# Attention values of a tile in two neighbouring PSUM banks, normalised in one step, with smaller key and value rings and a new instruction order

## The chip, the core and the metric

The kernel runs on one core of a Trainium2 chip. The metric is the device time of one execution in microseconds (us). The engines are TensorE (PE, matrix products into PSUM), VectorE (DVE), ScalarE (ACT), GpSimd (POOL, here mostly the issuer of loads that convert float32 to bfloat16 on the way) and SyncE (SP, here the issuer of transposing DMAs and of stores). They run side by side, each in the order of its own instruction stream, and wait for each other by semaphores.

## What is computed

```
scores = scale * q @ k.T                     # (4, 8, 768, 768), head size 64
keep   = is_global | is_local                # first 8 keys, or the last 96 positions
a      = softmax(where(keep, scores - slope[h] * dist, -1e9))
x      = (a @ v).transpose(0, 2, 1, 3).reshape(3072, 512)
out    = relu(x @ w_in) ** 2 @ w_out         # w_in 512 x 2048, w_out 2048 x 512
```

## The kernel before

**Tiles and blocks.** The 4 x 768 positions make 24 tiles of 128 rows (`j`), six to a batch; two tiles make a block of 256 rows (`blk`, 12 of them). The local window of 96 positions means that a tile meets only itself, the tile before it and 8 global keys.

**Attention of a tile.** Loads of q, k and v come from POOL (lines 330 and 334). For tiles 0 to 7 PE transposes q and k (`tr`, line 528) and ACT or DVE copies them out of PSUM (`T`, lines 453 and 455); from tile 8 on SP issues a transposing DMA (`T`, line 554). `sc` (line 618) makes the scores with 64-row products; tiles 6 and 7, 12 and 13, 18 and 19 are made in one go. `exp` (ACT, line 684) leaves PSUM, `mul` (DVE, line 709) applies mask and slope, `pv` (PE, line 767) multiplies by v. One `pv` is half a tile, four heads, in one PSUM bank of 4 x 65 columns; the 65th column of a head is the sum that the softmax divides by. `norm` (DVE, lines 797 and 798) is a reciprocal of four sums and a multiply of 4 x 64 values for each half, so two of each in a tile; it writes `x`. Then x is transposed, by PE for tiles 0 to 7 (`trx`, line 835) and by a DMA from SP after that (`xT`, line 859).

**The two layers.** Block 0 and half of block 1 go through `s1` (plain products with w_in, line 1081). The other blocks use a scheme with seven products in place of eight (`first_seven`, line 917): `xs` makes differences of halves of xT on DVE (line 939), `h` are the seven products of a half block (p1 to p7, line 967, eight matmuls each), `u` copies partial sums out of a bank that the next product then adds to, `c` adds them up and clips them at zero, `q` squares into `hs`. The second layer (`seven`) does the same with sums `sum` (line 1185), products `s2` (line 1230, four matmuls each piece), copies `part`, results `o` (line 1305) and stores `st` (line 1327).

**What sets the order.** `ORDER` is a long string. A word is an operation, `@A` or `@V` puts a choice of engine on ACT or DVE, and the digits after the colon are the PSUM banks. `Plan.run` emits the operations in that order, and each engine keeps its part of it. Operations also name buffers of rings: eight banks, 16 work buffers `buf`, `xT` 3, `hs` 3, `x` 2, transposed keys and queries `qkT` 12 (`NKT`), values 10 (`NV`). Three ring slots hold q and k from tile 6 on. A load of tile j from tile 9 on waits, by a small memset on DVE (`gate`, line 502), until the value slot that it takes has been read.

Of the kernel before, what the change touches and what calls it, by code (L numbers as in the profile page):

```python
# [62 lines left out]
trx.1:6 exp.3.0.1 exp.3.1.0:7 exp.3.0.0 ld.win.1.0 pv.2.0:2 pv.2.1:5 norm.2.0:0 norm.2.1 gv.2@V mul.3.0:8 sc.4.0:1037
exp.4.1.0:9 trx.2:2 ld.win.4.0 xT.1@A exp.4.1.1:a tr.1.5:4 tr.0.5:5 T.1.5@A exp.4.0.0 xT.2@A:1 mul.3.1:b pv.3.0:0
pv.3.1:6 T.0.5@A s1.0.1:7 norm.3.0:1 gk.4@V exp.4.0.1 norm.3.1 gv.3@A s1.0.1#2 trx.3:4 sc.5.0:0126 exp.5.0.1:c
exp.5.1.0:d s1.0.4:5 exp.5.1.1 E0.0 mul.4.0:e xT.3@V ld.v.4 mul.4.1:f ones.6 pv.4.0:3 s1.1.1:4 relu.0.4@V:2 exp.5.0.0
ld.win.3.0 s1.0.3:2 pv.4.1:1 relu.0.1@A:0 sq.0.1@A:0 gv.4@A s1.0.3#2 mul.5.1:1 s1.1.3:6 norm.4.0:0 norm.4.1 ld.win.2.0
ld.win.0.0 s1.0.0:5 relu.0.3@A:3 sq.0.3@A mul.5.0:5 gate.10 s1.0.2:0 trx.4:7 relu.1.1@A:4 sq.1.1@A:1 xs.1.0:0 ld.v.5
ld.win.2.1 pv.5.0:3 ld.win.0.1 pv.5.1:1 xs.1.1 ld.win.6.0 ld.win.7.0 ld.win.5.0 relu.1.3@A:7 norm.5.0:1 norm.5.1
ld.wout.3 s1.1.2:2 xT.4@A:2 relu.1.2@A:8 ld.wout.2 ld.wout.1 ld.wout.0 isum.0.0 s1.1.0:4 s1.0.2#2 trx.5:3 gate.14  # L70
xT.5@V relu.1.0@A:6 sq.1.2@A s1.0.0#2 xs.2.0:1 h.2.0.p1:1 sq.1.0@V sq.0.4@A u.2.0.1@A:b isum.3.0 sq.1.3@A xs.2.1
ld.wout.7 isum.0.1 s1.0.0#3 s1.0.6:6 gate.11 isum.1.0 isum.1.1 xs.1.2 s1.0.7:7 h.2.0.p2:2 c.2.0.c11:9 h.2.1.p1:3
# [5 lines left out]
h.1.1.p4 h.2.0.p4 wsum.0.1 s2.1.p1.0:0 T.8 c.2.0.c21@A:6 h.2.0.p3 h.2.1.p4 s2.0.p1.0:7 h.1.1.p3 sum.0.1 s2.0.p2.0:4
q.1.1.c22@A q.1.1.c11@A s2.0.p1.1 q.2.1.c22@A:2 q.2.0.c11@A part.0.p1@A:0 c.1.1.c21@A:c s2.0.p2.1 s2.1.p1.1 wsum.1.1
s2.0.p6.0 s2.0.p6.1 c.1.1.c12:7 tr.1.6:1 tr.0.6:6 part.1.p1@A:1 q.1.1.c21@A s2.1.p2.0:2 q.2.1.c11@A sum.0.3 wsum.2.1  # L80
part.0.p6@A:2 o.0.p2:a c.2.1.c21@A:2 s2.1.p2.1 wsum.3.1 wsum.3.0 T.1.6@V s2.0.p7.0 s2.0.p7.1 gate.12 s2.0.p5.0
q.1.1.c12@A s2.0.p5.1 c.2.0.c12:e load.9 part.0.p7@A:3 q.2.1.c12@A T.0.6@A q.2.0.c22@A o.0.p5:d s2.0.p4.0 s2.0.p4.1
q.2.0.c12@A o.0.p4@A sum.1.0:1 s2.0.p3.0 tr.0.7:3 gate.13 sum.1.1 s2.0.p3.1 o.1.p2:0 o.0.p3 sum.1.2 T.0.7@A tr.1.7:1
sum.2.2:0 sum.1.3 sum.2.0 T.1.7@A q.2.0.c21@A s2.1.p6.0 s2.1.p6.1 q.2.1.c21@A part.1.p6@A:0 sc.6.0:567341 exp.6.1.0:3
load.10 gk.7@A exp.6.0.0 s2.1.p5.0 s2.1.p7.0 s2.1.p7.1 mul.6.0:b exp.7.0.0:9 exp.7.1.0 part.1.p7@A:3 s2.2.p1.0:6
s2.1.p5.1 sum.2.1 exp.7.0.1:1 exp.7.1.1 o.1.p5:c mul.7.0:5 s2.2.p1.1 pv.6.0:5 norm.6.0:0 s2.1.p4.0 s2.1.p4.1 o.1.p4@A
pv.6.1:7 s2.1.p3.0 sc.8.0:3415 exp.8.0.1:7 part.2.p1@A:1 pv.7.0:0 s2.1.p3.1 mul.7.1:8 norm.6.1 T.9 pv.7.1:7 norm.7.0:1
norm.7.1 trx.6:1 exp.8.1.0:4 xT.6@V:0 exp.8.1.1 exp.8.0.0 s2.2.p6.0 s2.2.p6.1 o.1.p3 gate.15 trx.7:0 xT.7@A gk.8@V
mul.8.1:f h.3.1.p1:4 u.3.1.1@A:e gv.7@V h.3.0.p2:7 sc.9.0:5132 exp.9.0.1:6 exp.9.1.0:2 xs.3.0:0 xs.3.1 exp.9.0.0
h.3.0.p1:0 h.3.1.p6 mul.8.0:3 s2.2.p2.0:3 u.3.0.1@V:9 pv.8.0:1 u.3.1.2@A:b T.10 c.3.0.c11:1 h.3.0.p6 pv.8.1:5  # L90
norm.8.0:0 exp.9.1.1 sum.2.3 norm.8.1 xs.3.2 part.2.p6@A:2 xT.8:2 s2.2.p2.1 h.3.1.p7 h.3.1.p5:7 u.3.0.2@A:5
u.3.1.3@A:8 c.3.1.c22:7 o.2.p2:4 mul.9.0:3 mul.9.1:9 h.3.0.p7 s2.2.p7.0 s2.2.p7.1 u.3.0.3@A:f q.3.1.c22@A:0
part.2.p7@A:3 q.3.0.c11@A h.3.0.p5:2 h.3.1.p2:1 c.3.1.c11:8 gv.8@V load.11 c.3.0.c22:7 h.3.1.p3 h.3.0.p4 c.3.0.c21@A:2
h.3.1.p4 c.3.1.c21@A:1 q.3.1.c11@A c.3.1.c12:6 s2.2.p5.0 pv.9.0:5 gk.9@V T.11 st.0.0 norm.9.0:1 q.3.1.c12@A
q.3.0.c22@A h.3.0.p3 pv.9.1:1 gv.9@A c.3.0.c12:e norm.9.1 s2.3.p1.0:0 s2.2.p5.1 sc.10.0:4752 exp.10.1.1:f h.4.0.p1:1
s2.2.p4.0 exp.10.1.0:3 s2.2.p4.1 q.3.0.c12@V s2.3.p1.1 sum.3.0:1 o.2.p5:b s2.2.p3.0 s2.2.p3.1 exp.10.0.1 exp.10.0.0
part.3.p1@A:0 sum.3.1 h.4.1.p1:2 s2.3.p6.0 o.2.p4@A mul.10.0:8 s2.3.p6.1 sum.3.2 pv.10.0:7 mul.10.1:9 o.2.p3 gk.10@A
xT.9 norm.10.0:0 xs.4.0:1 xs.4.1 h.4.1.p2:5 pv.10.1:4 q.3.1.c21@A q.3.0.c21@A part.3.p6@A:1 u.4.1.1@A:6 u.4.0.1@A:5
s2.3.p7.0 s2.3.p7.1 h.4.1.p6 u.4.1.2@A:7 norm.10.1 h.4.0.p6 u.4.0.2@A:e gate.18 sc.11.0:6374 exp.11.1.0:a exp.11.0.0
gv.10@V c.4.1.c11:3 part.3.p7@V:3 sum.3.3 xs.4.2 load.12 h.4.0.p2:5 T.12 exp.11.1.1:1 h.4.1.p7 s2.3.p4.0 mul.11.0:2  # L100
exp.11.0.1 c.4.0.c11:f u.4.1.3@A:8 mul.11.1:9 load.13 h.4.0.p7 h.4.1.p5:3 c.4.1.c22:6 s2.3.p2.0:6 pv.11.0:4
u.4.0.3@A:a norm.11.0:1 q.4.1.c11@A:1 h.4.1.p4 h.4.0.p5:7 c.4.0.c22:5 s2.3.p2.1 o.3.p2:2 pv.11.1:5 q.4.1.c22@A
h.4.1.p3 q.4.0.c11@A gate.16 norm.11.1 h.4.0.p4 c.4.1.c21@A:1 c.4.0.c21@A:3 h.4.0.p3 s2.3.p4.1 c.4.1.c12:8 q.4.1.c12@A
c.4.0.c12:6 T.13 s2.3.p5.0 s2.3.p5.1 o.3.p5:9 q.4.0.c22@A q.4.0.c21@A o.3.p4@A sc.12.0:425137 exp.12.0.0:a st.2.1
exp.12.1.0 exp.13.0.0:b exp.13.1.0 exp.13.0.1:f q.4.0.c12@V s2.3.p3.0 sum.4.2:0 sum.4.0 xT.10:1 h.5.1.p1:0 s2.3.p3.1
mul.12.0:7 s2.4.p1.0:4 xT.11 o.3.p3 gate.19 xs.5.0:0 xs.5.1 h.5.0.p1:2 u.5.0.1@A:e q.4.1.c21@A h.5.1.p2:5 s2.4.p1.1
sum.4.1 part.4.p1@A:2 u.5.1.1@A:8 load.15 load.14 st.2.0 st.3.1 h.5.0.p5:1 pv.12.0:6 h.5.0.p6 mul.13.0:5 h.5.0.p2:3
c.5.0.c11:3 norm.12.0:0 s2.4.p6.0 xs.5.2 u.5.0.2@A:6 exp.13.1.1 mul.13.1:a q.5.0.c11@A:2 h.5.1.p6 h.5.0.p7 pv.12.1:7
u.5.0.3@A:4 s2.4.p2.0:3 s2.4.p6.1 s2.4.p2.1 pv.13.0:6 c.5.0.c22:1 gk.13@V h.5.0.p3 u.5.1.2@A:9 c.5.1.c11:b h.5.0.p4
norm.13.0:1 q.5.0.c22@A part.4.p6@A:0 norm.12.1 pv.13.1:5 norm.13.1 o.4.p2:e h.5.1.p7 gate.21 c.5.0.c12:3 h.5.1.p5:6  # L110
s2.4.p7.0 s2.4.p7.1 c.5.0.c21@A:7 q.5.0.c21@A u.5.1.3@A:f load.16 st.1.0 T.14 q.5.1.c11@V c.5.1.c22:0 h.5.1.p4 T.15
sum.4.3 T.16 sc.14.0:7251 xT.12:0 gv.13@A xT.13 q.5.1.c22@V q.5.0.c12@A s2.4.p5.0 part.4.p7@A:3 gate.17 exp.14.1.0:4
# [1337 lines left out]
```

## Time and profile before

| | |
|---|---|
| timed runs | 197.23 us median of 3 (196.97 to 197.88) |
| span of the profiled execution, first to last instruction | 195.7 us |
| PE busy | 188.5 us, 2808 matmuls |
| DVE busy | 179.4 us, 437 instructions |
| ACT busy | 161.6 us, 338 instructions |
| granted TensorE clock | 1.00 throughout |

The profiled execution's own total is not listed beside its span; the median of the timed runs is 1.5 us more than the span, and this is taken as what lies around it. A view "by line" groups equal instructions: busy time, mean duration of one, and how long the engine stood idle before them and for whom. In the timeline and in the chain a row begins with start and duration in us. Matmul records overlap, so that a busy PE need not be one that issues without a gap; a group's pace is read from starts.

### The profile page before, as it was taken

What the parts mean: (1) busy time and instruction counts of PE and PEld (TensorE: products, weight loads), DVE (VectorE), ACT (ScalarE), POOL (GpSimd) and SP (SyncE); (2) the same over time, 40 slices, a digit from 0 to 9 for tenths busy, and PEclk for the clock granted to TensorE, in tenths of its full rate; (3) what the DMA queues carried; (4) which work ended last, traced back from release to release, by engine and by line L of the source; (5) the groups of instructions that cost most, each with busy time, mean ns of one, the idle gap of its engine ahead of it and who ended that gap; (6) DMA issues with size and microseconds to landing.
All of it is one profiled execution on the core that took longest, in us unless ns stands there. A gap on an engine that the chain in (4) does not pass through costs nothing.

```text
span 195.7 us, 6835 instructions
## 1 busy us (share of the span) xinstructions
PE 188.5 (96%) x2808; PEld 170.5 (87%) x2808; DVE 179.4 (92%) x437; ACT 161.6 (83%) x338; POOL 75.1 (38%) x93
## 2 busy tenths in 40 slices
...
GB/s 125 149 150 167 179 193 205 205 162 151 155 150 143 99 177 168 119 100 227 139 79 129 138 74 119 209 168 97 147 113 188 85 136 13 20 193 105 0 91 234
DMA packets 111713, 26.92 MB, mean 138 GB/s; under 512 B 103234, under 2 KB 108866, under 8 KB 111682
## 3 DMA queue, kind: packets, MB, share of 16 engines
...
q8 instruction: 22, 0.36, 0.7%
...
## 4 chain that ended last, share of the span: by engine, by line
PE 85%; POOL 6%; DMA 5%; DVE 1%; issue 0%; POOLq 0%; DVEq 0%
PE bank L1230 37%; PE bank L967 32%; PE bank L1081 6%; PE bank L618 5%; PE bank L767 5%; POOL qk_first L330 5%; DMA win<-in_moe_w_in_dram 3%; DMA xT<-x 2%; POOL v L330 2%; PE bank L835 1%; PE bank L528 0%; DVE xs L939 0%; DVE buf L886 0%; DVE hsum L1185 0%; DVE early L1305 0%
## 5 line engine op out<-in xcount | busy, mean ns | idle before, releaser
L684 ACT ACTIVATE buf<-bank 128x512 bf16<-128x512 f32 x76 | 41.5, 613 | 2.8 <-PE bank L618 2.7
L1031 ACT ACTIVATE hs<-buf 128x512 bf16<-128x512 f32 x62 | 37.2, 635 | 2.5 <-DVE buf L1011 2.0
L1230 PEld LDWEIGHTS <-hsum 128*128 128x128 bf16 x384 | 35.3, 98 | 4.0
L453 ACT COPY buf<-bank 128x512 f32<-128x512 f32 (+1 forms) x59 | 32.1, 569 | 7.7 <-PE bank L967 6.1
L1230 PE MATMUL bank<-wsum,hsum 128*128 128x256 bf16 x288 | 38.0, 273 | 0.0
L1011 DVE CUSTOM_DVE_ANT_0 buf<-bank,buf 128x512 f32<-128x512 f32 x49 | 33.0, 682 | 0.8 <-ACT buf L453 0.3
L967 PEld LDWEIGHTS <-qk_first 128*128 128x128 bf16 x504 | 31.1, 98 | 1.4 <-issue 0.3
L967 PEld LDWEIGHTS <-win 128*128 128x128 bf16 x504 | 30.8, 98 | 0.9
L334 POOL DMA_DIRECT2D qk<-in_q_dram x18 | 16.0, 889 | 35.3 <-DMA qkT<-qk 30.0
L1230 PEld LDWEIGHTS <-hs 128*128 128x128 bf16 x288 | 26.3, 98 | 2.7
L1230 PE MATMUL bank<-wout,hs 128*128 128x256 bf16 x192 | 27.3, 273 | 0.0
L334 POOL DMA_DIRECT2D v<-in_v_dram x18 | 16.0, 891 | 23.1 <-PE bank L967 13.1
L967 PE MATMUL bank<-xs,qk_first 128*128 128x128 bf16 x336 | 24.6, 219 | 0.2 <-DVE buf L886 0.2
L967 PE MATMUL bank<-xT,win 128*128 128x128 bf16 x336 | 24.6, 219 | 0.0
L709 DVE TENSOR_TENSOR buf<-buf,E 128x1024 bf16<-128x1024 bf16 x32 | 21.5, 683 | 0.5 <-ACT buf L684 0.5
L798 DVE TENSOR_TENSOR x<-bank,rs 128x256 bf16<-128x256 f32 x48 | 20.4, 425 | 1.7
L767 PE MATMUL bank<-v,buf 128*128 128x65 bf16 x312 | 16.1, 193 | 0.9 <-DMA v<-in_v_dram 0.5
L1185 DVE TENSOR_TENSOR hsum<-hs 128x1024 bf16<-128x1024 bf16 (+1 forms) x26 | 16.4, 642 | 0.3
L334 POOL DMA_DIRECT2D qk<-in_k_dram x18 | 16.1, 897 | 0.6 <-DMA wout<-in_moe_w_out_dram 0.4
L767 PEld LDWEIGHTS <-buf 128*128 128x128 bf16 x312 | 13.9, 98 | 1.8 <-DVE buf L709 0.6
L884 ACT ACTIVATE buf<-bank 128x512 f32<-128x512 f32 x23 | 13.7, 607 | 1.0 <-PE bank L967 1.0
L453 ACT COPY part<-bank 128x256 f32<-128x256 f32 x29 | 11.1, 383 | 3.6 <-PE bank L1230 3.6
...
## 6 DMA issues: line engine op xcount, KB each, us to landing
...
```

The source lines that it names most:

```text
L334: nc.gpsimd.dma_start(out=dst, in_=src)
L453: nc.scalar.copy(dst, src)
L684: nc.scalar.activation(out=tiles[tag, j, g][:, odd], in_=tiles.pop(("sc", j, odd, g)).rearrange("p a c -> p (a c)"), func=Act.Exp, scale=s ...
L709: nc.vector.tensor_mul(at, tiles.pop(("esc", j, g)), bias)
L767: nc.tensor.matmul(out=po[:, hi, :], lhsT=tiles["at", j, g][:, odd, at * P : (at + 1) * P], rhs=v_sb[kj][:, h, :], start=(i == 0), stop=(i ...
L798: nc.vector.tensor_tensor(out=x[:, 4 * hf : 4 * hf + 4, :], in0=po[:, :, :D], in1=rs.to_broadcast([P, 4, D]), op=Alu.mult,)
L884: nc.scalar.activation(dst, src, Act.Relu)
L967: nc.tensor.matmul(out=tiles["h", blk, g, bank][:, n], lhsT=left_[:, s, k], rhs=right_[:, k], start=opens and n == 0 and k == 0, stop=k == ...
L1011: nc.vector._custom_dve(TENSOR_ADD_SAT, out=hr, in0=src, in1=tiles.pop(("u", blk, g, i)), s0=float("inf"), s1=0.0,)
L1031: nc.scalar.activation(hs, hr, Act.Square)
L1185: nc.vector.tensor_tensor(out=t[:, i, h], in0=t[:, a, h] if isinstance(a, int) else half_a(blk, *a)[:, h], in1=t[:, b, h] if isinstance(b, ...
L1230: nc.tensor.matmul(out=tiles["acc", blk, bank][:, cols], lhsT=left_[:, s], rhs=right_[:, cols], start=first and s == 0, stop=s == NSTEP - ...
```

## The change

1. `pv` of both halves of a tile takes two neighbouring banks at once (all banks are now one PSUM tile), and one `norm` follows: a reciprocal of 8 sums and a multiply of 8 x 64 values, read across the two banks. Both banks stay taken until it is through.
2. `NKT` goes from 12 to 9 and `NV` from 10 to 9; `hs` and `xT` rings go from 3 to 4 buffers.
3. `ORDER` is another string: the order of all operations, the choices of engine and the banks.
4. `first_seven` can take two blocks at a time; with `PAIRS` empty this isn't used, and its products are as before.

```diff
-    NQ, NKT, NV = 3, 2 * TPB, 10
+    NQ, NKT, NV = 3, 9, 9
-    banks = [ps.tile([P, 4 * P], FP32, name=f"bank_{i}", tag=f"bank_{i}") for i in range(NBANK)]
+    bank_all = ps.tile([P, NBANK, 4 * P], FP32, name="bank", tag="bank")
+    banks = [bank_all[:, i] for i in range(NBANK)]
-    NHB = 3
+    WHOLE = True
+    PAIRS = ()
+    NHB = 4
+    NXT = 4
...
-                po = psum()[:, : 4 * (D + 1)].rearrange("p (a c) -> p a c", a=4)
+                if hf == 0 and WHOLE:
+                    assert given[1] == given[0] + 1
+                    tiles["po", j] = bank_all[:, given[0] : given[0] + 2, : 4 * (D + 1)].rearrange("p b (a c) -> p b a c", a=4)
+                po = tiles["po", j][:, hf] if WHOLE else psum()[:, : 4 * (D + 1)].rearrange("p (a c) -> p a c", a=4)
...
+            def emit_whole(e, j=j):
+                tiles["x", j] = lent("x")
+                x, po = tiles["x", j], tiles.pop(("po", j))
+                rs = work.tile([P, 2, 4, 1], FP32, name="rs", tag="rs")
+                nc.vector.reciprocal(rs, po[:, :, :, D : D + 1])
+                nc.vector.tensor_tensor(
+                    out=x.rearrange("p (b a) c -> p b a c", b=2),
+                    in0=po[:, :, :, :D],
+                    in1=rs.to_broadcast([P, 2, 4, D]),
+                    op=Alu.mult,
+                )
```

The order of the start in both, from the first operation to the first one with w_in (`ld` is a load's issue on POOL, `s1.0.1` the first product with w_in):

```diff
-tr.0.0:0 T.0.0@V tr.1.0:1 bias.0.0:23 T.1.0@V ld.q.1 ld.k.1 tr.0.1:4 T.0.1@V ld.q.2 ld.k.2 E0.1 ld.q.3 ld.v.0 ld.k.3
-tr.1.1:5 T.1.1@A ld.v.1 sc.0.0 bias.1.0:6701 exp.0.1.0:0 sc.1.0 tr.0.2:4 exp.0.0.0 gk.1@A T.0.2@V exp.1.0.0:1 tr.1.2:5
...
+tr.0.0:0 T.0.0@A tr.1.0:1 bias.0.0:23 T.1.0@A ld.q.1 tr.0.1:0 ld.k.1 tr.1.1:4 T.1.1 T.0.1 sc.0.0 exp.0.0.0:0 exp.0.1.0
+bias.1.0:1567 sc.1.0 gk.1 exp.1.0.0:1 E0.1 ld.q.2 ld.v.0 tr.0.2:3 T.0.2 ld.k.2 tr.1.2:2 T.1.2 pv.0.0:01 pv.0.1 norm.0:0
+exp.1.1.0 exp.1.1.1:3 ld.k.4 tr.1.4:5 T.1.4 exp.1.0.1 bias.2.0:4372 ones.6 sc.2.0 exp.2.0.0:2 ld.q.3 tr.0.3:5 T.0.3
+exp.2.1.0 trx.0:0 xT.0:0 gk.2@A exp.2.0.1:0 ld.k.3 tr.1.3:1 T.1.3 exp.2.1.1 ld.v.1 pv.1.0:45 pv.1.1 norm.1:0 sc.3.0:1036
+exp.3.1.0:3 ld.q.4 tr.0.4:7 T.0.4 gv.1 ld.v.2 pv.2.0:45 pv.2.1 gk.3 exp.3.0.0 mul.3.0:1 exp.3.0.1:4 exp.3.1.1 norm.2:1
+gv.2 ld.q.5 ld.k.5 trx.1:1 xT.1@A sc.4.0:3702 exp.4.1.1:3 exp.4.0.0:0 tr.0.5:6 T.0.5 tr.1.5:1 ld.v.3 gk.4@A exp.4.0.1
+trx.2:4 xT.2@A:1 pv.3.0:56 mul.3.1:2 pv.3.1 T.1.5 sc.5.0:1032 exp.5.0.0:2 exp.4.1.0 ld.win.1.0 s1.0.1:4 ld.win.3.0
+norm.3:1 trx.3:5 xT.3 s1.0.1#2
```

The new order of PE and SP around three later places that the prediction speaks of (other engines left out; a word without a piece number stands for one piece of four matmuls of `s2` or eight of `h`):

```
tile 9:   tr.1.6 tr.0.6 tr.1.7 s2.0.p4 s2.0.p4 s2.0.p3 s2.0.p3 tr.0.7 s2.1.p2 s2.1.p6 s2.1.p6 sc.6 (with 7) s2.1.p7 s2.1.p7
          s2.2.p1 s2.1.p5 s2.1.p5 s2.1.p4 s2.1.p4 pv.6.0 pv.6.1 s2.1.p3 s2.1.p3 st.0.1 T.8 sc.8 pv.7.0 s2.2.p1 trx.6 pv.7.1
          s2.2.p2 s2.2.p2 s2.2.p6 trx.7 T.9 sc.9
block 7:  s2.4.p3 (last piece) ... pv.14.0 pv.14.1 ... pv.15.0 pv.15.1 ... st.4.0 T.17 sc.17 xT.14 xT.15 h.7.1.p1
block 9:  pv.19.0 pv.19.1 s2.7.p3 s2.7.p3 T.21 sc.21 s2.8.p1 xT.18 h.9.0.p1 st.3.1 st.4.1 xT.19 h.9.0.p2 s2.8.p2 s2.8.p6 s2.8.p6
          h.9.1.p1 pv.20.0 pv.20.1 s2.8.p7 s2.8.p7 h.9.0.p6
```

More of the change, by code (lines that the diff above doesn't have):

```diff
@@ L63 @@
[L63 to L72, printed above, removed]
@@ L78 @@
[L78 to L87, printed above, removed]
@@ L88 @@
[L88 to L112, printed above, removed]
@@ new lines @@
+part.1.p7@V:1 s2.1.p4.0 gk.7@A exp.6.1.0:7 exp.6.0.0 sum.2.0:0 exp.7.1.1 mul.6.0:d exp.7.1.0:6 o.1.p5:4 exp.7.0.0
+mul.7.0:7 s2.1.p4.1 o.1.p4 pv.6.0:01 pv.6.1 norm.6:1 s2.1.p3.0 s2.1.p3.1 o.1.p3 q.2.1.c21 load.8 st.0.1 T.8 sc.8.0:7365
+mul.7.1:3 pv.7.0:01 s2.2.p1.1 trx.6:2 sum.2.1 pv.7.1 norm.7:1 exp.8.0.1:6 exp.8.1.1 mul.8.1:3 s2.2.p2.0:6 gv.7
+part.2.p1:2 s2.2.p2.1 o.2.p2:6 s2.2.p6.0 gk.8@A exp.8.1.0:c xT.6@A:2 exp.8.0.0 sum.2.2 load.9 trx.7:0 xT.7@A xs.3.0:0
+mul.8.0:7 xs.3.1 xs.3.2 T.9 sc.9.0:2135 exp.9.0.1:d exp.9.1.0:5 exp.9.0.0 mul.9.0:c h.3.1.p1:7 u.3.1.1:9 h.3.0.p1:0
@@ L303 @@
     }
+    xs_all = const([P, 2, 4 * 2 * P], BF16, "xs")
+    buffers["xs"] = [xs_all[:, i].rearrange("p (z k c) -> p z k c", z=4, k=2) for i in range(2)]
     buffers["buf"] = [early[:, i] for i in range(3)] + buffers["buf"]
@@ L782 @@
                 key=base + 2 + 2 * hf,
-                takes=(*G, [users]),
+                takes=(*G, [users] if not WHOLE else both) if hf == 0 or not WHOLE else None,
             )
+            if WHOLE and hf == 0:
+                p_["adj"] = 2
             mul_users[g].append(p_)
@@ L790 @@
             users.append(p_)
+            def emit_whole(e, j=j):
[9 more added lines that the diff above has]
+                )
+            if WHOLE:
+                if hf == 1:
+                    n_ = plan.op(
+                        ("norm", j), vec(0.82), emit_whole, deps=pvs, key=base + 4.3, takes=("x", 2, [xusers]),
+                    )
+                    for us in both:
+                        us.append(n_)
+                    xusers.append(n_)
+                    norm.append(n_)
+                continue
             def emit_norm(e, j=j, hf=hf):
```

272 lines of the change are left out of this document (158 added, 114 removed).

## The prediction

> **What bounds the kernel now.** I read the page's head first, then busy time by stretches, then the chain of work that ended last.
>
> ```profile
> span 195.7 us, 6835 instructions
> PE 188.5 (96%) x2808; PEld 170.5 (87%) x2808; DVE 179.4 (92%) x437; ACT 161.6 (83%) x338; POOL 75.1 (38%) x93
> ...
> PE 85%; POOL 6%; DMA 5%; DVE 1%; issue 0%; POOLq 0%; DVEq 0%
> ```
>
> ```profile
> 0.00:21.44 21.44, 17.74 (x257) 12.84 (x257) 16.52 (x58) 17.35 (x38) 20.10 (x29) 1.00 1.82 151
> 21.44:128.00 106.56, 106.56 (x1641) 98.69 (x1638) 101.60 (x245) 95.91 (x200) 47.98 (x57) 1.00 1.57 151
> 128.00:130.00 2.00, 1.81 (x25) 1.61 (x23) 1.99 (x4) 1.71 (x4) 0.00 (x0) 1.00 1.08 97
> 130.00:192.20 62.20, 62.20 (x896) 57.36 (x892) 58.83 (x131) 46.62 (x97) 6.99 (x8) 1.00 0.60 109
> 192.20:195.70 3.50, 0.20 (x2) 0.00 (x0) 0.42 (x1) 0.00 (x0) 0.00 (x0) 1.00 0.50 176
> ```
>
> After the stretch's bounds and length come the busy times of PE, weight loads, DVE, ACT and POOL. PE is busy without a gap from 21.44 to 192.2 us but for 0.2 us near 129. Its holes are the start, 21.44 - 17.74 = 3.7 us, and the end, 3.3 us. DVE is nearly as full in the middle (101.60 of 106.56, 95%), but the chain gives it 1%: what DVE does is late almost nowhere. A change that adds no product can gain what is left of those holes, and it can lose at any place where a result comes later than PE asks for it.
>
> The holes of the start, in the timeline of PE:
>
> ```profile
> 15.77 0.65 PE L767 MATMUL bank<-v,buf 128*128 128x65 bf16 x16 [0.49 <-DMA v<-in_v_dram]
> ...
> 18.40 0.40 PE L767 MATMUL bank<-v,buf 128*128 128x65 bf16 x8 [0.21 <-ACT buf L684]
> 18.98 0.42 PE L767 MATMUL bank<-v,buf 128*128 128x65 bf16 x8 [0.17 <-DVE buf L709]
> 19.66 1.07 PE L1081 MATMUL bank<-xT,win 128*128 128x128 bf16 x16 [0.27 <-DMA win<-in_moe_w_in_dram]
> ...
> 21.44 1.05 PE L1081 MATMUL bank<-xT,win 128*128 128x256 bf16 x8
> ```
>
> Two landings bound it: v of tile 2 at 15.77 and the first piece of w_in at 19.66. POOL issues the same 14 loads ahead of that piece in both orders (only their order changes), so it lands at the same time in both.
>
> **Part 1: one norm a tile.** Prices, by line and shape (busy, mean ns of one):
>
> ```profile
> L1011 DVE CUSTOM_DVE_ANT_0 buf<-bank,buf 128x512 f32<-128x512 f32 x49 | 33.0, 682 | 0.8 <-ACT buf L453 0.3 <-PE bank L967 0.3
> L453 ACT COPY buf<-bank 128x512 f32<-128x512 f32 x51 | 29.3, 600 | 6.2 <-PE bank L967 6.1
> L798 DVE TENSOR_TENSOR x<-bank,rs 128x256 bf16<-128x256 f32 x48 | 20.4, 425 | 1.7
> L1305 DVE TENSOR_TENSOR buf<-bank,part 128x256 f32<-128x256 f32 x25 | 10.4, 418 | 1.2 <-PE bank L1230 1.0
> L797 DVE RECIPROCAL rs<-bank 128x4 f32<-128x4 f32 x48 | 8.7, 180 | 0.6
> L455 DVE COPY buf<-bank 128x512 f32<-128x512 f32 x4 | 2.7, 684 | 0.0
> ```
>
> 48 reciprocals and 48 multiplies go: 48 x (0.180 + 0.425) = 29.0 us. 24 of each come. A multiply of 512 values over two banks is not in the trace; the nearest rows, 512 values out of one bank, take 0.682 and 0.684. I take 0.683; at most it could cost two of the old ones, 0.85. A reciprocal of 8 sums lies between 0.180 and, at most, two of them, 0.36; I take 0.185. Sum 24 x 0.868 = 20.8 us: **8.2 us of DVE go**, between 0 (if two banks cost as much as two instructions) and 8.2.
>
> [...]
>
> **Part 2: what the new order gives back.** Counting the two instruction streams, DVE goes from 439 to 404 and ACT from 340 to 326: beside the 48 that norm loses, DVE gains 13 and ACT loses 14. The large ones are 6 squarings, 3 copies of 512 values, 3 small ones of 256, 3 copies of global values and one of a transpose. DVE gets about 9 x 0.683 + 3 x 0.418 = 7.4 us for the first three kinds and some 0.4 net for the rest; ACT loses about 14 x 0.6 = 8 us. So **DVE stays at about 179 us and ACT falls to about 154**. PE keeps its 2808 matmuls and 21 stretches of scores. Neither engine ends the span, so this saving by itself is worth nothing on the clock; what it hides behind is PE. Were PE's cover gone, DVE, at 95% in the middle, would take over about 5% below the present time.
>
> **Part 3: smaller rings.** A load of tile j now waits for the values of tile j-9 instead of j-10, and `T` of tile j for the keys of tile j-9. The closest case is tile 15, which takes the place of tile 6, whose values are read as global ones until gv.10, after some 70 us of PE work (about 75 us):
>
> ```profile
> 66.28 0.91 POOL L334 DMA_DIRECT2D v<-in_v_dram  x1
> 77.13 0.88 POOL L334 DMA_DIRECT2D qk<-in_q_dram  x1 [9.95 <-DMA qkT<-qk]
> ```
>
> Its v went out at 66.28, its q not before 77.13, since a q and k slot (three in both) came free only then. So v may go 9 us later and still be ahead of q; behind it on POOL stands only that q. Cost nothing. Larger `hs` and `xT` rings take no wait away that the trace shows: nothing.
>
> **Part 4: norm waits for both halves.** x of a tile is complete later after its last `pv`. The pace of DVE is read from starts:
>
> ```profile
> 16.21 0.18 DVE L797 RECIPROCAL rs<-bank 128x4 f32<-128x4 f32 x1
> 16.43 0.42 DVE L798 TENSOR_TENSOR x<-bank,rs 128x256 bf16<-128x256 f32 x1
> 16.77 0.17 DVE L797 RECIPROCAL rs<-bank 128x4 f32<-128x4 f32 x1
> ```
>
> An old half takes 16.77 - 16.21 = 0.56 us, the new whole about 0.22 + 0.61 = 0.83: 0.27 us later for each tile, on the way to `xT`. Two banks of eight stay taken meanwhile. On PE's path this counts only where xT is late (below): 0 to 0.27 each, taken as 0.
>
> **Part 5: the start.** At 21.44 the old order has done both pieces of `s1.0.1`, `trx.3` and `sc.5`; the new one has done exactly the same work when the second piece of `s1.0.1` ends. After pv.2 (end 15.77 + 0.65 = 16.42), DVE has norm.2, gv.2, T.0.5, mul.3.1 and T.1.5 ahead of sc.5: 0.83 + 0.3 + 0.34 + 0.61 + 0.4 = 2.5 us, so sc.5 at 18.9 to 19.3 (the later if gk.3 and mul.3.0 run past pv.2), `s1.0.1` at 19.66 to 20.0, trx.3 behind norm.3 at 20.1 to 20.5, second piece over at **20.8 to 21.15**: 0.3 to 0.65 us sooner. Against it: the new order puts the transposes of tile 4 ahead of tile 2's scores, so ACT stands idle for about a us near 11.5; the sum above holds since later exps wait for v and k anyway. I take -0.5, and +0.4 as the other end.
>
> **Part 6: later arrivals.** The wait near 129 is block 8's:
>
> ```profile
> 120.72 0.44 PE bank L1230 x4
> 121.16 0.45 PE bank L967 x8
> ...
> 123.03 4.44 DMA xT<-x
> ...
> 127.55 0.44 DVE xs L939
> 128.01 0.29 DVE xs L939
> ...
> 129.56 1.95 PE bank L967 x32
> ```
>
> Here a transposing DMA took 4.44 us. Counting the new PE order with 0.44 for a piece of `s2` and 0.45 for one of `h`, 8.9 us of PE work lie between the last pv of block 8 and its first product with differences, against 8.0 before: this wait goes, -0.3.
>
> Tile 9 in the timeline:
>
> ```profile
> 45.41 0.61 PE L528 MATMUL bank<-ident,qk 128*128 128x128 bf16 x8
> ...
> 60.49 0.23 PE L618 MATMUL bank<-qkT 64*128 64x128 bf16 x2
> ```
>
> ```profile
> 46.31 0.88 POOL L334 DMA_DIRECT2D qk<-in_q_dram  x1 [2.01 <-PE bank L528]
> ...
> 58.20 0.88 POOL L334 DMA_DIRECT2D qk<-in_q_dram  x1 [1.21 <-DMA qkT<-qk]
> ```
>
> Tile 6's slot is free when its transposes end (46.02); then q and k of tile 9 load and are transposed, and POOL, which waited for that, goes on at 58.20: at most 12.2 us. The old order had 60.49 - 46.02 = 14.5 us of PE work over it. The new one has 20 pieces of `s2` (8.75), three transposes not yet done and two of x (1.0), scores of 6, 7 and 8 (1.5) and pv of 6 and 7 (0.7): 11.9 us. So tile 9's scores are late by about 0.3 us: +0.3. Other places (block 7 behind T.17, block 9 behind two stores) come out at a margin of 0 to 2 us; +0.15 for all of them.
>
> The tail has the same last pieces, copies and quarter stores: 0.
>
> **Sum.** -0.5 (start) - 0.3 (block 8) + 0.3 (tile 9) + 0.15 = -0.35 us. On the span 195.35; on the median, 1.5 above the span, **196.9**.
>
> **Rivals.** *Slower: transposing DMAs land late where the order is tight.* Issues and medians to landing:
>
> ```profile
> qkT<-qk SPq DMA_TRANSPOSE x16, 5.2
> xT<-x SPq DMA_TRANSPOSE x16, 2.7
> ```
>
> xT took 2.7 at the median and 4.44 in block 8: one is easily 1.7 us later than another. In block 9 the new order leaves 6.0 us of PE work between pv.19 and h.9.0.p6 (7.3 before), for norm (0.9), two store issues and xT (2.7 to 4.4) and xs (0.8): 4.4 to 6.1 and what the stores' 512 KB hold up, some 1 to 2 us. In block 7 xT.14 stands on SP behind T.17, and that behind st.4.0. From the point at which a landing passes 12 us at tile 9 or 6 us at block 9, each us is a us of PE. A us at two of the three and a half at the last: +2.5 - 0.35, **199.4**. For it: margins near zero in the new order at places that had 1 to 2 us. Against: the loads that slow these DMAs are over by block 9 (POOL is nearly idle from 130 us on).
>
> [...]
>
> *Faster: DVE was the brake of the start, and of small waits.* The floor of the start is w_in at 19.66, two pieces and trx.3: 20.8. With block 8's wait gone and tile 9 in time: -0.65 - 0.3 = -0.95, **196.2** or a little less. Against it: ACT's idle time in the start.
>
> *A two-bank operand is no cheaper than two.* Then DVE has 8 us more, 187 in all; near 98% full in the middle it makes PE wait in places, by about 1 us: **198.3**.
>
> **Chances.** Forecast and its own range 196.3 to 198.2: 0.45. Late landings: 0.30. Two-bank price: 0.05. Faster start and more: 0.20. About 0.5%, 1 us, is what a measurement of this kernel can tell from no change; so faster by more 0.20, within 0.45, slower by more 0.35. The range 195.8 to 199.7 leaves out a start better than the floor and landings worse than two late ones.
>
> **What would show it.** In the new profile: a two-bank multiply near 0.683 us, DVE near 179 and ACT near 154 us busy; PE without a gap from 21 us, its start holes 0.3 to 0.65 smaller; scores of tile 9 waiting up to half a us for a transpose; no wait in block 8. Wrong would be: gaps of PE behind xT or qkT of a us or more (the slower rival), waits of PE for DVE in the middle, or a first product with w_in later than 20.5.

## The result and the profile after

| | before | after |
|---|---|---|
| median of the runs, us | 197.10 (4 runs, 196.94 to 197.88) | 209.12 (4 runs, 207.25 to 211.71) |
| span of the profiled execution, us | 195.7 | 207.8 (the execution took 209.57) |
| mean granted clock of PE in it | 1.00 | 0.992 |
| DVE, ACT busy, us | 179.4, 161.6 | 178.2, 157.3 |

The changed kernel is slower: ratio 1.057, 95% interval 1.051 to 1.062. The forecast was 196.9, the range ended at 199.7. The prediction was wrong by 12 us. One of the four executions after, 211.71, and one of the four of run 11 below were in a slower state, and the ratios leave them out.

The page's head and the two groups of the new norm:

```profile
span 207.8 us, 6845 instructions
...
PE 191.1 (92%) x2808; PEld 172.1 (83%) x2808; DVE 178.2 (86%) x402; ACT 157.3 (76%) x324; POOL 75.0 (36%) x93
...
PE 71%; DMA 16%; POOL 5%; ACT 3%; DVE 2%; issue 2%; SPq 0%; DVEq 0%; POOLq 0%
```

```profile
L802 DVE TENSOR_TENSOR x<-bank,rs 128x512 bf16<-128x512 f32 x24 | 16.6, 692 | 0.8
L801 DVE RECIPROCAL rs<-bank 128x8 f32<-128x8 f32 x24 | 4.8, 200 | 2.3 <-PE bank L767 2.3
```

The multiply over two banks takes 0.692 us, and DVE's total is what was forecast. But in the chain that ended last DMA has risen from 5% to 16%. Busy time by stretches (stretch, its length, then PE, weight loads, DVE, ACT, POOL, and the granted clock):

```profile
0.00:21.44 21.44, 18.28 (x261) 13.77 (x262) 15.34 (x55) 16.83 (x37) 20.63 (x30) 1.00 1.86 154
21.44:56.00 34.56, 34.56 (x479) 32.20 (x477) 33.89 (x71) 31.18 (x64) 21.11 (x27) 1.00 1.61 169
56.00:60.00 4.00, 2.20 (x44) 1.75 (x42) 2.60 (x6) 1.37 (x4) 1.14 (x2) 1.00 2.38 141
...
89.00:96.00 7.00, 3.81 (x36) 2.92 (x34) 4.28 (x10) 3.01 (x7) 0.00 (x0) 0.76 0.07 16
...
121.00:125.00 4.00, 0.88 (x23) 0.78 (x21) 1.69 (x5) 1.27 (x3) 0.00 (x0) 1.00 1.28 80
125.00:138.00 13.00, 12.99 (x202) 12.26 (x199) 12.22 (x27) 8.62 (x17) 0.88 (x1) 1.00 0.82 62
138.00:140.00 2.00, 0.90 (x14) 0.74 (x12) 2.00 (x7) 0.88 (x3) 0.00 (x0) 1.00 0.56 119
...
157.00:159.00 2.00, 1.08 (x15) 0.78 (x14) 1.97 (x4) 1.56 (x5) 0.00 (x0) 1.00 0.66 237
```

PE, which had one hole of 0.2 us between 21 and 192 us, now has five: 4.00 - 2.20 = 1.8 us near 56, 3.2 near 89, 3.1 near 121, 1.1 near 138 and 0.9 near 157, together 10.1. PE's busy time has grown by 191.1 - 188.5 = 2.6 us at the same 2808 products; in the stretch with the hole at 89 the clock granted is 0.76. The start is 0.5 better (holes of 21.44 - 18.28 = 3.16 instead of 3.70). 9.9 + 2.6 - 0.5 + 0.1 is the 12.1 us between the spans. The fall of the clock is the smaller part: two of the other executions of the changed kernel ran at a granted clock of 1.00, with spans of 205.4 and 206.9.

What PE and DVE waited for there, in the view of waits (engine and line, what it waited for, us in total, times, longest):

```profile
DVE xs L981 <- DMA xT<-x: 8.0, 3, 4.3
PE bank L767 <- DVE v L451: 3.7, 2, 3.1
PE bank L1272 <- DVE hsum L1227: 3.2, 1, 3.2
PE bank L614 <- DMA qkT<-qk: 1.8, 1, 1.8
PE bank L1012 <- DMA xT<-x: 0.9, 1, 0.9
```

The hole at 89 step by step, from the timelines of SP, DVE and PE:

```profile
84.75 1.19 SPq L887 DMA_TRANSPOSE xT<-x  x1
```

```profile
85.80 0.68 DVE L1081 TENSOR_TENSOR hs<-buf 128x512 bf16<-128x512 f32 x1
90.82 0.42 DVE L981 TENSOR_TENSOR xs<-xT 128x512 bf16<-128x512 bf16 x1 [4.33 <-DMA xT<-x]
...
91.49 0.42 DVE L1347 TENSOR_TENSOR buf<-bank,part 128x256 f32<-128x256 f32 x1
91.82 0.68 DVE L1227 TENSOR_TENSOR hsum<-hs,hsum 128x1024 bf16<-128x1024 bf16 x1
```

```profile
92.56 0.82 PE L1272 MATMUL bank<-wout,hsum 128*128 128x256 bf16 x3 [3.19 <-DVE hsum L1227]
```

SP issues xT of tile 11 at 84.75; DVE can use it only at 90.82, some 6 us later. DVE comes to `xs.5.0` at 86.5 and stands there for 4.33 us. What PE lacks isn't the difference: it is the sum `sum.3.3` (91.82), which has its inputs and stands behind `xs` in DVE's order. The hole at 121 is the same with `xs.7.0`, tile 15 and `gv.15`. The one at 56 begins in SP's queue:

```profile
50.48 0.39 SPq L1369 DMA_DIRECT2D out_dram<-buf  x1
50.97 1.59 SPq L550 DMA_TRANSPOSE qkT<-qk  x1
```

```profile
58.37 0.23 PE L614 MATMUL bank<-qkT 64*128 64x128 bf16 x2 [1.80 <-DMA qkT<-qk]
```

The new order puts a store, `st.0.1`, ahead of `T.8`. SP stands at the store until its copy is done, and `T.8` goes at 50.97, beside the store's 256 KB and loads; the scores of tile 8 start at 58.37, 7.4 us after the issue. Before, it went at 48.91 and landed 4.9 us later:

```profile
48.91 1.33 SPq L554 DMA_TRANSPOSE qkT<-qk  x1
```

### The profile page after: what moved, and what is told of

Same layout as the page of the kernel before. It is cut to its first block, busy times and chain, and to the rows that moved or that the text cites. A ratio compares the mean times of both kernels' runs of the same rounds, so it can differ in the third digit from the quotient of the medians.

```text
span 207.8 us, 6845 instructions
## 1 busy us (share of the span) xinstructions
PE 191.1 (92%) x2808; PEld 172.1 (83%) x2808; DVE 178.2 (86%) x402; ACT 157.3 (76%) x324; POOL 75.0 (36%) x93
## 4 chain that ended last, share of the span: by engine, by line
PE 71%; DMA 16%; POOL 5%; ACT 3%; DVE 2%; issue 2%; SPq 0%; DVEq 0%; POOLq 0%
PE bank L1272 28%; PE bank L1012 28%; DMA xT<-x 8%; PE bank L1133 5%; PE bank L767 5%; PE bank L614 4%; DMA qkT<-qk 4%; POOL qk_first L326 3%; DMA qk_first<-in_q_dram 2%; DMA out_dram<-buf 2%; ACT hs L1079 1%; POOL v L326 1%; PE bank L863 1%; ACT qkT L449 1%; ACT buf L449 1%
## 5 line engine op out<-in xcount | busy, mean ns | idle before, releaser
L1272 PEld LDWEIGHTS <-hsum 128*128 128x128 bf16 x384 | 35.9, 99 | 7.6 <-DVE hsum L1227 3.4
L680 ACT ACTIVATE buf<-bank 128x512 bf16<-128x512 f32 x68 | 37.6, 612 | 3.5 <-PE bank L614 2.6
L1272 PE MATMUL bank<-wsum,hsum 128*128 128x256 bf16 x288 | 38.2, 273 | 0.0
L449 ACT COPY buf<-bank 128x512 f32<-128x512 f32 (+1 forms) x48 | 25.9, 567 | 13.9 <-PE bank L1012 6.8
L1079 ACT ACTIVATE hs<-buf 128x512 bf16<-128x512 f32 x56 | 33.7, 636 | 2.3 <-DVE buf L1057 2.2
L1057 DVE CUSTOM_DVE_ANT_0 buf<-bank,buf 128x512 f32<-128x512 f32 x43 | 28.9, 683 | 1.5 <-ACT buf L449 0.8
L1272 PEld LDWEIGHTS <-hs 128*128 128x128 bf16 x288 | 26.8, 98 | 3.1
L1272 PE MATMUL bank<-wout,hs 128*128 128x256 bf16 x192 | 26.4, 275 | 0.0
L802 DVE TENSOR_TENSOR x<-bank,rs 128x512 bf16<-128x512 f32 x24 | 16.6, 692 | 0.8
L1272 PE MATMUL bank<-wout,hsum 128*128 128x256 bf16 x96 | 13.8, 285 | 3.2 <-DVE hsum L1227 3.2
L912 ACT ACTIVATE buf<-bank 128x512 f32<-128x512 f32 x21 | 12.6, 598 | 4.9 <-PE bank L1012 3.4
L705 DVE TENSOR_TENSOR buf<-buf,E 128x1024 bf16<-128x1024 bf16 x22 | 15.0, 684 | 0.6 <-ACT buf L680 0.6
L614 PEld LDWEIGHTS <-qkT 64*128 64x128 bf16 x352 | 9.9, 94 | 5.6 <-issue 2.3
## 6 DMA issues: line engine op xcount, KB each, us to landing
wout<-in_moe_w_out_dram POOLq DMA_DIRECT2D x8, 256.0 KB, 10.1
```

Source lines behind the costliest of these rows:

```text
L449: nc.scalar.copy(dst, src)
L614: nc.tensor.matmul(out=tiles["sc", j, odd, g][:, at, :], lhsT=left[j - 1][half, pair, :] if kt else qkT[j % NKT][half, 1, pair, :], rhs=qk ...
L680: nc.scalar.activation(out=tiles[tag, j, g][:, odd], in_=tiles.pop(("sc", j, odd, g)).rearrange("p a c -> p (a c)"), func=Act.Exp, scale=s ...
L705: nc.vector.tensor_mul(at, tiles.pop(("esc", j, g)), bias)
L802: nc.vector.tensor_tensor(out=x.rearrange("p (b a) c -> p b a c", b=2), in0=po[:, :, :, :D], in1=rs.to_broadcast([P, 2, 4, D]), op=Alu.mult,)
L912: nc.scalar.activation(dst, src, Act.Relu)
```

## The experiments

All times are medians, all ratios are to the kernel before in the same runs, with 95% intervals.

| run | us | ratio |
|---|---|---|
| 1 wide norm, old order | 213.9 | 1.081 (1.075 to 1.086) |
| 2 same, neighbouring banks | 205.7 | 1.036 (1.026 to 1.045) |
| 3 new bank numbers alone, halves | 203.6 | 1.026 (1.018 to 1.033) |
| 4 halves, new order | 214.2 | 1.079 (1.070 to 1.089) |
| 5 new order, ten value slots | 209.3 | 1.058 (1.053 to 1.064) |
| 6 old order, nine value slots | 198.6 | 1.006 (1.003 to 1.010) |
| 7 new order, `xs` later | 208.3 | 1.052 (1.046 to 1.059) |
| 8 new order, no loads from tile 14 on | 204.5 | 1.033 (1.027 to 1.039) |
| 9 new order, `st.0.1` behind `T.8` | 214.1 | 1.086 (1.080 to 1.092) |
| 10 new order, six places | 206.4 | 1.041 (1.030 to 1.053) |
| 11 new order, four places | 203.3 | 1.028 (1.023 to 1.033) |
| 12 new order, stores later | 202.2 | 1.022 (1.017 to 1.027) |
| 13 new order, no loads from tile 9 on | 200.8 | 1.014 (1.008 to 1.020) |
| 14 new order, no stores of blocks 0 to 6 | 208.8 | 1.051 (1.044 to 1.059) |

**Parts of the change alone (1 to 6).**

Run 1 takes the old order and merges the two norms of 19 tiles:

```diff
-norm.4.0:0 norm.4.1
+norm.4:0            # in0 = bank_all[:, b0 : b1 + 1 : b1 - b0]
```

> The order of before, with the wide norm (one reciprocal, one multiply over two banks, here also two banks that aren't neighbours) for 19 of the 24 tiles, at the place of the second half's norm; tiles 6, 12, 14, 16 and 17 keep two halves, since a bank is used again between their two norms. DVE loses 19 x (0.605 x 2 - 0.868) = 6.5 us. Theory 1 (the wide norm is harmless and worth nothing on the clock, the loss is the order's): 196.5 to 198, and a multiply near 0.69. Rival (x that is complete 0.27 us later and banks held longer make PE wait): 200 or more, with PE waiting for xT or for banks.

213.9 us, as the rival had it, but the waits show another reason:

```profile
PE bank L1256 <- DVE x L802: 4.3, 4, 1.4
DVE rs L801 <- ACT buf L683: 3.9, 3, 2.2
DVE rs L801 <- PE bank L1107: 2.4, 1, 2.4
```

Products of the second layer (L1256) wait for the wide multiply, and its reciprocal for an exponential and for products with w_in. None of them use its values. The waits fit a program that orders instructions by the stretch of PSUM that an operand spans, so that an operand with halves in banks 1 and 5 also holds banks 2 to 4: the second piece of `s2.2.p2`, in bank 3, starts at 73.32, 1.30 us late, right behind the multiply of tile 8, whose halves lie in banks 1 and 5. So run 1 doesn't tell the price of the wide norm. Runs 2 and 3 number the old order's banks anew so that halves are neighbours, with and without the wide norm:

```diff
-pv.4.0:3 ... pv.4.1:1
+pv.4.0:b ... pv.4.1:b+1     (every bank of the order is chosen anew)
```

> The order of before with its banks numbered anew, so that the two halves of 19 tiles lie in neighbouring banks, and the wide norm for these 19 (tiles 6, 12, 14, 16 and 17 keep halves). The run before it with banks up to five apart showed PE and DVE waiting for banks that lay between the two. If those waits made its 16 us, and the wide norm itself is harmless: DVE 6.5 us less, no waits between the wide multiply and other banks, 196.5 to 198.5. If the wide norm itself costs (x later, banks held longer): 203 or more.

> The control of the run above: the kernel before with the same new numbers of banks, all norms in halves. 197 to 198 if the numbering costs nothing; what it costs is to be taken off the run above.

New bank numbers alone cost about 5 us (203.6), which no theory expected. In run 3 the largest of PE's new waits behind the start are for ACT's exponentials (L683):

```profile
PE bank L966 <- ACT buf L683: 1.2, 3, 0.6
PE bank L766 <- ACT buf L683: 1.0, 2, 0.6
```

The products of the first layer (L966) use no value of an exponential; what they can wait for is the bank that it still reads. In the kernel before, the list of PE's waits has one for an exponential, of 0.2 us. From 22 us on PE's holes are 3.8 us in all, where the kernel before has 0.2.

The wide norm adds 2.1 us (205.7). Its waits show where:

```profile
PEld L861 <- DVE x L802: 2.2, 4, 0.8
```

PE waits for x in its own transposes (L861), or, for 0.7 us in the second layer and 0.6 in the first, for a bank that the multiply still holds. So in an order made for halves the wide norm is a small loss, and the time that DVE gains (busy 175.3 us instead of 179.3 in run 3) is worth nothing.

Run 4 is the reverse, the new order with halves:

```diff
-    WHOLE = True
+    WHOLE = False          # norm.j:x -> norm.j.0:x norm.j.1; banks as they are
```

> The changed kernel with the norm in two halves at the place of the wide one, same order, same banks: 24 x (1.210 - 0.877) = 8 us more of DVE. Theory 1 (the loss is the order's, the wide norm earns its 8 us of DVE): the holes at 56, 89, 121, 139 and 157 us stay, with DVE at about 186, 209 to 213. Rival (the wide norm makes the loss): 200 or less.

```profile
L829 DVE TENSOR_TENSOR x<-bank,rs 128x256 bf16<-128x256 f32 x48 | 20.4, 425 | 2.2 <-PE bank L866 0.5
L828 DVE RECIPROCAL rs<-bank 128x4 f32<-128x4 f32 x48 | 8.3, 172 | 2.4 <-PE bank L770 2.4
```

28.7 us of DVE for the norm instead of 21.4, and the ratio rises from 1.057 to 1.079, 4 to 5 us. The holes stay (its waits name `xs` behind xT with 7.2 us, scores behind qkT with 3.3). The wide norm isn't what costs; in the new order it earns.

Runs 5 and 6 change the ring of values:

```diff
-    NQ, NKT, NV = 3, 9, 9        -    NQ, NKT, NV = 3, 2 * TPB, 10
+    NQ, NKT, NV = 3, 9, 10       +    NQ, NKT, NV = 3, 2 * TPB, 9
```

> The changed kernel with ten value slots again (the fourth xT buffer, which its order never uses, makes room); the DVE marks that let the loads of tiles 15 and 21 go stand earlier, behind norm.6 and norm.12. Theory 2 (the smaller value ring delays v of tile 15 from 66 to 80 us, so that six loads run into xT of tile 11): that load goes out near 68, the other five from 77 to 82, xT of tile 11 lands in about 4 us instead of 5.97, PE's hole of 3.35 us at 89 falls to 1.5 or less: 206 to 207.5, the holes at 56, 121, 139 and 157 stay. Theory 1 (the order alone): the five loads wait for q and k slots anyway, hole as before, 208.5 to 209.5.

> The kernel before with nine value slots instead of ten, the DVE marks of tiles 15 and 21 behind gv.10 and gv.16. Theory 1 (the smaller ring costs nothing to speak of): 197 to 198.5. Theory 2 (it bunches the loads and delays transposes): v of tile 15 goes at 75 to 80 instead of 66, holes of PE near 89 or 93, 200 or more.

The tenth slot in the new order doesn't change the time, but it moves the holes. v of tile 15 goes out at 70.53 instead of 80.19, five loads in place of six run ahead of xT of tile 11, and that lands in 3.7 us instead of 6.0:

```profile
70.53 0.92 POOL L330 DMA_DIRECT2D v<-in_v_dram  x1
91.38 0.43 DVE L981 TENSOR_TENSOR xs<-xT 128x512 bf16<-128x512 bf16 x1 [2.02 <-DMA xT<-x]
```

PE's hole at 89 shrinks from 3.2 to 0.9 us, as theory 2 had it. But the hole at 56, ahead of the load that moved, is 3.1 here instead of 1.8, the clock is at half rate for 3.4 us behind it, and a new hole of 0.9 opens at 111. So theory 2 is right about the place and wrong about the time. In the old order nine slots show 198.6, a ratio of 1.006, with v of tile 15 at 78.42 instead of 66.28. That isn't clearly a cost of the ring: its profiled execution has the span and the holes of the kernel before (195.5 us, 0.2 behind 22 us), and the kernel before itself ran in 196.9 to 199.9 us in these comparisons.

**DVE's order (7).** Three words of the changed order move:

```diff
-xT.10:2 xT.11 xs.5.0:0 xs.5.1 s2.3.p5.1 o.3.p5:4 sum.3.3 ... o.3.p3 xs.5.2
+xT.10:2 xT.11 s2.3.p5.1 o.3.p5:4 sum.3.3 ... o.3.p3 xs.5.0:0 xs.5.1 xs.5.2
-xs.7.0:1 exp.17.1.0 mul.17.0:a ... gv.15 ... gv.16 xs.7.1
+exp.17.1.0 mul.17.0:a ... gv.15 ... gv.16 xs.7.0:1 xs.7.1
```

> The changed kernel with three words moved in the order: the first differences xs.5.0 and xs.5.1 stand right ahead of xs.5.2, xs.7.0 right ahead of xs.7.1; nothing else. Theory 3 (DVE, which works in order, stands at xs for a late xT, and what stands behind it, sum.3.3 at 89 us and mul.17.0 and gv.15 at 121 us, is what PE lacks): the holes of 3.35 and 3.29 us fall to 0 to 1 us each, 203 to 205. Rival (PE needs xs itself just as soon, DVE's order doesn't matter): the holes move by less than 1 us, 207.5 or more.

The two holes are gone (the stretches that hold them, and the one at 56):

```profile
56.00:60.00 4.00, 0.82 (x11) 0.50 (x11) 2.81 (x6) 0.54 (x2) 0.00 (x0) 1.00 1.93 146
60.00:66.00 6.00, 6.00 (x82) 4.91 (x81) 3.12 (x8) 3.95 (x9) 4.38 (x5) 0.72 1.85 139
66.00:111.00 45.00, 44.80 (x720) 41.33 (x718) 42.06 (x97) 39.07 (x82) 14.02 (x16) 1.00 1.38 143
111.00:113.00 2.00, 1.10 (x21) 0.78 (x21) 2.00 (x5) 1.14 (x4) 0.00 (x0) 1.00 1.29 109
```

From 66 to 111 us PE lacks 0.2, where 3.2 was lost. So theory 3 is right about these two places: standing DVE turned a late transfer into a hole. But the time falls by only 0.9, to 208.3. In its profiled execution (206.95 us) the hole at 56 is 3.2 instead of 1.8, `T.8` being slower, six us at clock 0.72 follow it, and a new one of 0.9 opens at 111. The words that moved stand behind 56, so the longer hole there isn't their doing: up to there the instructions are those of the changed kernel. The size of that hole differs from execution to execution (1.8 in the changed kernel, 3.2 here, 2.5 in run 8), which blurs what a mended place is worth.

**The traffic beside the transposes (8, 13, 14).** Run 8 leaves out loads, at an unchanged order:

```diff
         def emit_load(e, j=j):
+            if j >= 14:          # run 13: j >= 9
+                return
```

> The changed kernel without POOL's loads of q, k and v for tiles 14 to 23 (30 of its 86 DMAs): these tiles are worked out from what older tiles left in the slots; every other instruction stays. Theory 4 (the transposing DMAs are slow because loads are in flight): xT of tiles 11 and 15 land in 2.4 to 3 us instead of 5.97 and 6.55, the holes at 89 and 121 go, the one at 56 stays: 200 to 203. Rival (they're slow by themselves, or by the stores beside them): the landings stay over 4 us, 206 or more.

204.5 us. xT of tile 11, out at 87.56, is there for DVE at 90.12, after 2.56 us instead of 6.07:

```profile
87.56 1.19 SPq L889 DMA_TRANSPOSE xT<-x  x1
90.12 0.42 DVE L983 TENSOR_TENSOR xs<-xT 128x512 bf16<-128x512 bf16 x1 [0.83 <-DMA xT<-x]
```

Its figure lies above the 200 to 203 that was expected: the hole at 56, which had been left in, is 2.5 instead of 1.8 with 3.4 us at half rate behind it, and holes of 0.5, 0.7 and 1.0 stay at 120, 134 and 153. Loads and stores are told apart by runs 13 and 14:

> The changed kernel without POOL's loads of q, k and v for tiles 9 to 23: these tiles are worked out from what older tiles left in the slots; its order and everything else stay, the stores too. Theory A (the holes after 50 us come from loads in flight beside the transposes): T.8 and all xT land in 2.4 to 4.5 us, the holes at 56, 89 and 121 go, those of the stores (139, 157) stay at 1.0 to 1.3: 197.5 to 200. Theory B (the stores make as much of it): 203 or more.

> The changed kernel without the stores of blocks 0 to 6 (14 of 26; these rows of the output aren't written); order, loads and everything else stay. Theory A (loads): the holes at 139 and 157 and the one of T.8 at 56 go, those at 89 and 121 stay at 3 us each, 203 to 206. Theory B (stores make as much of it): 89 and 121 shrink to 1.5 or less as well, 199 to 202.

Run 13 by stretches:

```profile
22.00:130.00 108.00, 107.65 (x1658) 99.73 (x1657) 103.32 (x224) 94.31 (x194) 15.48 (x20) 1.00 0.74 103
130.00:132.50 2.50, 1.37 (x21) 1.20 (x20) 2.50 (x7) 1.28 (x3) 0.00 (x0) 1.00 0.72 162
...
151.00:153.50 2.50, 1.29 (x16) 1.05 (x15) 1.56 (x5) 1.57 (x4) 0.00 (x0) 1.00 0.63 119
```

Without loads the new order keeps PE busy for 107.65 of 108 us; two holes, 1.1 and 1.2, are left. Where `T.8`, xT of tile 11 and xT of tile 15 took 7.4, 6.0 and 6.5 us to land, they take 3.4, 2.5 and 3.7. None of the five holes is a wait for a load itself. So loads that fly beside the transposes make most of the 12 us: 1.057 becomes 1.014 without them. The loads aren't new, though: before, `T.10` took 6.5 us and xT of tile 14 5.5, and PE had 0.2 us of holes. What the new order lost is the room for such landings.

Without early stores (run 14) the holes at 89 and 121 stay, `PE bank L1272 <- DVE hsum` at 2.9 us and `PE bank L767 <- DVE v` at 2.9; the one at 56 goes, with 0.6 at 60 in its place, and the one at 138 goes, which was ACT's wait for the buffer of a store. 208.8 is above what either theory gave: a hole of 0.9 opens at 111, the clock is twice at half rate for 3.4 us, and the hole at 157, expected to go with the stores, stays at 1.1. So that one isn't the stores'. Its transpose, xT of tile 18, takes 4.1 us in run 14 with neither a load nor a store beside it, and the next one 2.4. What does fall between its issue and its landing are two DMAs of a kind that the profile calls "instruction" (packets, MB, share of 16 engines):

```profile
q8 instruction: 1, 0.02, 1.5%
q14 instruction: 1, 0.01, 0.5%
```

In run 12, where it takes 4.2 us, the one of q8 alone is there. In run 13 that one comes 2.3 us behind the issue of xT of tile 18, which takes 2.4 us beside two stores; xT of tile 19, with it, takes 4.0 and lands at 153.0, when the hole of 1.2 ends. None of the runs moves these DMAs alone, so whether they delay the transpose isn't shown.

**Mending single places (9 to 12).** Run 9 takes only the store from in front of `T.8`:

```diff
-st.0.1 T.8
+T.8 st.0.1
```

> The changed kernel with one word moved: the store st.0.1 stands behind T.8 in SP's queue instead of ahead of it. In the changed kernel SP stands at that store until 50.48, T.8 goes out at 50.97 instead of 48.91 as before, flies beside the store's 256 KB and a run of loads, lands 7.36 us later, and the scores of tile 8 make the hole at 56. Theory 6 (the store in SP's queue makes this hole): T.8 out near 48.9, landed by 55, the hole gone: 205 to 206.5. Rival (T.8 is slow by the loads alone): hole of 1.5 us or more, 208 or more.

`T.8` lands in time and its hole goes. But the store now flies beside `T.9`:

```profile
53.99 5.19 SPq L551 DMA_TRANSPOSE qkT<-qk  x2
```

```profile
62.91 0.23 PE L615 MATMUL bank<-qkT 64*128 64x128 bf16 x2 [2.86 <-DMA qkT<-qk]
```

The scores of tile 9 start at 62.91, 8.9 us after `T.9` went out; the hole of `gv.15` grew to 4.8. 214.1 us. `T.9` is as slow in runs 5 and 7 (9.1 us), where the store stands ahead of `T.8` and the longer hole at 56 gives it the time. The hole moved on, and theory 6 is right about the place and wrong about the time. Run 10 mends six places at once (the differences as in run 7; `st.0.1` behind `T.10`; the scores of tile 9 later; a free buffer for `u.8.1.1`; `st.3.1` and `st.4.1` behind `xT.19`):

```diff
-u.8.1.1:f        +u.8.1.1:e
-st.0.1 T.8 ... T.10              +T.8 ... T.10 st.0.1
-xT.18:0 ... st.3.1 st.4.1 ... xT.19      +xT.18:0 ... xT.19 st.3.1 st.4.1
```

> The changed kernel with the differences later (as in the run before), and four more places of its order mended: the scores of tile 9 stand 0.9 us of PE work later; the store st.0.1, whose 256 KB fly beside T.9, goes behind T.10; u.8.1.1 takes a work buffer that is free instead of the one that st.5.0 has just begun to store; st.3.1 and st.4.1 go behind xT.19 instead of between it and xT.18. Theory 5 (the loss is a sum of single places at which a transfer has less time than it needs, each mended by itself): the holes at 56 (3.34 and 1.2 at the lower clock), 136 (1.2) and 155 (1.1) go to 0.5 or less each, 199 to 202. Rival (a hole that is mended comes back elsewhere, since the transfers as a whole are too slow for this order): 205 or more.

206.4. Here `st.0.1` sends what a later step has left in its buffer (128 rows of the output), and SP stood at it until 71.66, so that xT came late; new holes stood at 75 and 156. Runs 11 and 12 avoid this:

```diff
 run 11: T.8 st.0.1 ...; xs later; u.8.1.1:e; ... T.20 st.3.1 st.4.1 ...
 run 12: o.0.p5:e; T.10 st.0.1 ...; xT.19 st.6.1 ...; sc.9.0 behind u.3.0.1; the rest as in run 11
```

> The changed kernel with st.0.1 behind T.8, the differences xs.5.0, xs.5.1 and xs.7.0 later (as in the run on DVE's order), u.8.1.1 in a work buffer that is free, and st.3.1 and st.4.1 (ready since 100 us) behind T.20 instead of right behind xT.18. In the run with six places holes came back at 75 (st.0.1 then stood behind T.10 and held SP up until 71.66) and at 156 (exp.21.0.1 waited for the buffer of st.3.1), which these edits avoid. Theory 5 (single places, each mended by itself): holes at 56, 89, 121, 136 and 155 of 0.7 us or less, 198.5 to 201.5. Rival (they come back elsewhere): 204 or more.

> The changed kernel with the edits of the run with four mended places, and its two remaining holes taken up. In that run T.8 landed in time, but T.9 flew beside st.0.1 and took 8.03 us (hole of 2.65 at 60), and T.21 flew beside st.6.1 and took 8.44 (holes of 1.0 and 1.1 at 151 to 153). Here st.0.1 goes behind T.10 (its tile in a work buffer that nothing else uses until then, so that the store holds nothing up), st.6.1 behind xT.19, and the scores of tile 9 stand 0.9 us of PE work later. Theory 5 (single places, most of them stores put where transposes and loads are in flight): no hole over 0.9 us after 22 us, 198 to 200.5. Rival (holes come back elsewhere, the loads alone are enough): 202.5 or more.

203.3 and 202.2. Run 12 by three stretches that still lose:

```profile
60.00:66.00 6.00, 5.20 (x93) 4.56 (x91) 4.56 (x12) 5.42 (x12) 3.26 (x4) 1.00 1.51 204
...
118.00:121.00 3.00, 2.21 (x29) 1.93 (x28) 2.47 (x8) 1.56 (x4) 0.00 (x0) 1.00 1.37 86
...
149.00:152.00 3.00, 1.85 (x36) 1.45 (x30) 2.97 (x5) 2.62 (x7) 0.00 (x0) 1.00 0.42 113
```

Words moved, with the same loads, the same rings and the same norm, give back 7 of the 12 us; each remaining hole is 1.2 us or less. Theory 5 and its rival are both half right. Of the 4.7 us that run 12's span is above the one before, holes from 22 us on are 2.7, PE's busy time 1.4 (189.9 instead of 188.5, at the full clock; why is open) and the start 0.4. No version beat the kernel before.

## Why the prediction was wrong, point by point

- **Part 1, the norm: right.** 24 x (0.692 + 0.200) = 21.4 us against 29.0, 7.6 saved; the multiply was put at 0.683, and the reciprocal of 8 sums, for which the kernel before has no row, at 0.185.
- **Part 2, the engines: DVE right, ACT not.** DVE ended at 178.2 (about 179 forecast). ACT ended at 157.3 (154 forecast): it fell by 4.3 us, not by 8. Nothing in the sum hung on it.
- **Part 3, the rings: right in the sum, not in the reasoning.** No change of time in the new order (run 5), a ratio of 1.006 in the old one (run 6), inside the spread of the kernel before. But I said that v may go 9 us later at no cost; it went into a run of six loads that slowed xT of tile 11 (run 5).
- **Part 4, x later by 0.27 for each tile, taken as 0:** 2.1 us in the old order (run 2 against run 3); in the new one the saving outweighs it (run 4).
- **Part 5, the start: right.** -0.5 forecast, 3.70 to 3.16 measured; the first product with w_in starts at 19.94, within the 19.66 to 20.0 of the sum.
- **Part 6, block 8's wait goes: right.** PE is busy for 12.99 of the 13 us from 125 to 138.
- **Part 6, tile 9 late by 0.3: wrong place.** I followed tile 9's slot from PE's transposes over POOL to `T.9`. What was late was tile 8, by 1.8 us, since `st.0.1` had been moved ahead of `T.8` in SP's queue. A DMA's place in its issuer's queue, and what flies beside it, was not counted for each DMA.
- **Part 6, "other places (block 7 behind T.17, block 9 behind two stores) come out at a margin of 0 to 2 us; +0.15 for all": this step failed.** The other places cost 3.2 (block 5, tile 11), 3.1 (block 7, tile 15), 1.1 (a work buffer taken again as soon as its store was issued, 138) and 0.9 (xT of tile 18, 157, landing after 3.9 us where the next one takes 2.4), and PE's busy time, at the lower clock among other things, 2.6 more. Two errors in it: I asked when PE would reach its own first product with differences, and not what stands behind `xs` in DVE's order (run 7); and I took landings of 2.7 to 4.4 us where the new order brings xT of tiles 11 and 15 among loads: 6.0 and 6.5 us.
- **The rival "transposing DMAs land late where the order is tight"** had the mechanism, and a price of 2.5 us. It counted only holes of PE behind transposes at three places, a us each; five places lost 10.1. Its "against" (block 9 lies behind the loads) held, and block 9 lost 0.9 all the same. The 1 to 2 us that it gave to the stores' 512 KB show in no run: without these stores the hole is 1.1 (run 14).
- **The two-bank rival's 198.3** doesn't follow from its own terms: 196.85 and about 1 us are 197.9. It played no part, since the multiply took 0.692.

What stays open: the part of run 3's 5 us that isn't a wait for an exponential, the 1.4 us of busy time in run 12, and why the hole at 56 differs between executions of the same instructions.
